# Linear attention ahead of two MLPs: the product with the state in four 64x64 parts, behind the state's own product

## The chip, the core and the metric

One core of a Trainium2 chip runs the whole program. The metric is the device time of one execution in microseconds (us); the inputs lie in HBM when it starts, and the output lies there when it ends. TensorE (PE) multiplies matrices and writes its results to PSUM; VectorE (DVE), ScalarE (ACT) and GpSimd (POOL) work element by element; SyncE (SP) issues the DMAs. [...]

## What is computed

The output of a causal linear attention with decay goes, token by token, through two MLPs. Only the attention is touched by the change. There are 2 batches of 8 heads, 768 tokens and 64 channels per head:

```python
for b in range(nb):
    intra = einsum(qb, kb) * Dmask          # scores inside a block
    intra = einsum(intra, vb)
    inter = einsum(qb * lam_pow, kv_state)  # the product with the state
    out[block] = intra + inter
    kv_state = lam_block * kv_state + einsum(kb * rev_pow, vb)
x = out as (1536 tokens, 512 features)
h = relu(x @ w_in); x = (s * h * h + b) @ w_out                   # first MLP, 2048 wide
x = rmsnorm(x); y = (silu(x @ w_gate) * (x @ w_val)) @ w_out2     # second MLP, 1536 wide
```

The kernel uses blocks ("chunks") of 128 tokens in place of 64, which gives the same result: 6 chunks per batch, 12 in all, numbered g = 0 to 11; chunk 0 and chunk 6 begin a batch with an empty state, and chunks 5 and 11 end one and leave no state behind.

## The kernel before, in words

The attention stage is a loop over the chunks, in `attention_moe_moe2_kernel`. Two heads share the 128 partitions ("a pair"): the upper 64 partitions hold the channels of an even head, the lower 64 those of an odd one. In each round g, the program gives TensorE this work, in this order (the order is written out by hand, and no scheduler changes it):

- `outputs(g)`, first part (line 558, tile `o`): values times masked scores, 8 products, one per head, with 128 tokens on the rows of the array and 64 channels on its columns (the trace writes 128*64), into one PSUM bank. Even and odd heads go to the two halves of the array's columns.
- `outputs(g)`, second part (line 567, tile `o`): the product with the state, 4 products, one per pair, 128*128. The state of a pair stands as a 128x128 block with the two heads' 64x64 states on its diagonal and zeros elsewhere. It adds to the same bank. Chunks 0 and 6 don't have it.
- `outputs(g)`, third part (line 584, tile `st`): the chunk's share of the new state, 8 products 128*64 of k scaled (`kdec`) with v. Chunks 5 and 11 don't have it.
- `scores(g + 2)` (line 516, tile `sc`): the scores of the chunk after the next, 8 products with 64 channels on the rows (64*128), into two banks.

The other engines work around it. ACT copies the bank `o` to x (line 578, one 128x512 operation; x of a batch is `xq`), and makes `kdec` of the next chunk (line 535, eight 128x64 operations, one per head). POOL makes q scaled (`qs`, line 530, 128x512) for the next chunk and scales the old state (line 546, 128x512). DVE adds the new share to the state (line 597, two 64x256 operations) and masks the scores of chunk g + 2 (`prob`, line 518, two 128x512 operations). The bank of `o` alternates between 4 and 5 with g, so a chunk's products need the copy of the chunk before the last.

From chunk 4 on, the loop also carries tasks for the first MLP, by a table `plan` keyed by g: splits of x into a high and a low part (lines 143 on ACT and 146 on DVE), and the unpacking of the first two blocks of weights (`w_tasks`). Unpacking reads a block that SP has fetched (line 116, a `st` buffer of 512 KB), takes two words from it on ACT (lines 123 and 129), shifts and adds them on DVE (lines 135 and 140), splits off the high part on ACT (line 143, 128x1024, tile `u`) and the low part on DVE (line 146). These tasks stand in the engines' queues between those of the attention. In round 11, two products of the first MLP (`hquad(0)`, line 295, tile `h`) stand ahead of `outputs(11)`.

SP issues the loads in order: chunk g + 4's q, k and kv (lines 442, 445, 450) at the end of round g, each as soon as its buffer is free; the kv buffer is free when chunk g's `st` is done. The first two blocks of weights (512 KB each, 4 KB per partition) go in behind chunk 8's loads, ahead of chunk 9's.

Of the kernel before, what the change touches and what calls it, by code (L numbers as in the profile page):

```python
# [15 lines left out]
P = 128  # L16
# [6 lines left out]
def attention_moe_moe2_kernel(  # L23
# [89 lines left out]
    raw = {}  # L113
# [60 lines left out]
    def load_w(j, part):  # L174
        if j < NPR:
            n = 4 * j + 2 * (1 - part)
        else:
            n = NU1 + 3 * (j - NPR) + 1 - part
        raw[j, part] = fetch(n, part)
# [150 lines left out]
    def hbanks(i):  # L330
        places = (7, 0, 6, 4) if i == 0 else tuple(4 * ((i + 1) % 2) + j for j in range(4))
        return [bank(n, f"h{i}_{j}")[:, 0:HB] for j, n in enumerate(places)]
# [104 lines left out]
    with tc.tile_pool(name="att", bufs=1) as att:  # L437
# [67 lines left out]
        qs, prob, state, o_bank = {}, {}, {}, {}  # L505
# [32 lines left out]
        def prepare_state(g):  # L538
            c = g % NCH
            if c == NCH - 1:  # L540
                return
            sn = att.tile([P, NPAIR, P], F32, tag="state", bufs=2, name=f"state{g}")
            if c == 0:
                nc.gpsimd.memset(sn, 0.0)
            else:
                nc.gpsimd.tensor_tensor(
                    sn, state[g - 1], lpow[:, :, P - 1 : P].to_broadcast([P, NPAIR, P]), op=ALU.mult
                )
            state[g] = sn

        def outputs(g):
# [3 lines left out]
            o = bank(4 + g % 2, f"o{g}")  # L555
            for h in range(H):
                pr = slice(h % 2 * D, (h % 2 + 1) * D)
                nc.tensor.matmul(  # L558
                    o[pr, h // 2 * P : (h // 2 + 1) * P],
                    vn[:, h, :],  # L560
                    prob[g][:, h, :],
                    start=h < 2,
                    stop=c == 0 and h >= H - 2,
                    skip_group_check=True,
                )
            for p in range(NPAIR if c else 0):
                nc.tensor.matmul(  # L567
                    o[:, p * P : (p + 1) * P],
                    state[g - 1][:, p],
                    qs[g][:, p],  # L570
                    start=False,
                    stop=p == NPAIR - 1,
                    skip_group_check=True,
                )
            o_bank[g] = o
            o3 = o.rearrange("p (a i) -> p a i", i=P)
            tok = slice(c * P, (c + 1) * P)
            nc.scalar.activation(xq[g // NCH][:, :, tok], o3, AF.Copy)
            if not last:
# [7 lines left out]
                return st  # L587
            return None

        def add_state(g, st):  # L590
            if st is None:
                return
            st3 = st[:, 0 : NPAIR * D].rearrange("p (a i) -> p a i", i=D)
            sn = state[g]
# [591 lines left out]
```

## Time and profile before

| | |
|---|---|
| device time, median of 3 runs | 594.74 us (594.52 to 595.35) |
| span of the profiled execution, first to last instruction | 592.7 us |
| attention stage in that execution, up to TensorE's long run of MLP products | 0 to 55.8 us |
| TensorE busy | 586.4 us, 99% of the span |
| DVE, ACT, POOL busy | 407.8, 321.5, 114.5 us |
| moved by DMA | 52 MB; 264 GB/s over the first 60 us |

The span is that of one execution, with times counted from its start. The time of a run is from outside and about 2 us more than a span, so a saving in the span is taken as the same saving in the time. In the trace a matmul of these types appears as two instructions (a product of two passes), so 8 products are 16 rows. Each row has a start and a duration; matmuls overlap, so the time of a group is read from its start to the start of the next group.

### The profile page before, as it was taken

Reading aid. Unit: us, or ns where it says so; the run is one execution under the profiler, and the core shown is the slowest. Engines: PE = TensorE matmul, PEld = TensorE weight load, DVE = VectorE, ACT = ScalarE, POOL = GpSimd, SP = SyncE. Lnnn points to the kernel's source line nnn. Section 1 sums busy time; section 2 is a strip of 40 time slices with the busy share of each in tenths; the row PEclk is TensorE's granted clock in tenths of the full one; section 3 lists DMA queues with packets and bytes.
Section 4 is the critical chain, followed back from the end, with each engine's and each line's share of the span. In section 5 each row is a group of like instructions: output and inputs, shape, how many; then the busy total and the mean of one; then the engine's idle time right before and its main releaser. Section 6 shows DMA issues by size and latency. Waiting matters only on the chain.

```text
span 592.7 us, 9212 instructions
## 1 busy us (share of the span) xinstructions
PE 586.4 (99%) x3590; PEld 543.1 (92%) x3590; DVE 407.8 (69%) x654; ACT 321.5 (54%) x572; POOL 114.5 (19%) x118
## 2 busy tenths in 40 slices
PE   9999999999999999999999999999999999999997
PEld 8888999999998888988888999999999998888886
DVE  6587957777777775769947986777777777874200
ACT  5677977777776663646542434444444445763200
POOL 3550032223103232041311002222222200000000
PEclk9999999999999999999999999999999999999999
DMA  8992202223223441221120001221222212320310
GB/s 312 334 350 72 72 1 78 77 72 131 72 72 110 139 143 35 71 69 38 36 72 1 1 2 71 72 72 71 72 72 71 86 58 77 136 72 1 142 38 35
DMA packets 17282, 51.98 MB, mean 88 GB/s; under 512 B 2390, under 2 KB 2390, under 8 KB 17238
## 3 DMA queue, kind: packets, MB, share of 16 engines
q1 hardware_dynamic: 17238, 51.39, 25.4%
q8 instruction: 28, 0.46, 0.3%
q14 instruction: 16, 0.13, 0.1%
HBM read 48.24 MB, written 3.15 MB: 87 GB/s over the span
## 4 chain that ended last, share of the span: by engine, by line
PE 93%; DVE 3%; ACT 2%; issue 1%; DVEq 0%
PE q L295 28%; PE h L295 17%; PE out L1078 17%; PE y L795 15%; PE z L807 8%; PE sc L516 2%; PE o L558 2%; PE o L567 2%; PE st L584 1%; PE warm L481 1%; PE rb L775 0%; DVE r_None L306 0%; PE nps L758 0%; DVE u_None L140 0%; ACT u_None L143 0%
## 5 line engine op out<-in xcount | busy, mean ns | idle before, releaser
L143 ACT ACTIVATE u_None<-u_None 128x768 fp32r<-128x768 f32 (+2 forms) x50 | 42.9, 871 | 55.0 <-DVE u_None L140 48.7
L295 PE MATMUL q<-u0b_None,u_None 128*128 128x384 f32 x360 | 68.4, 336 | 0.0
L295 PEld LDWEIGHTS q<-u0b_None,u_None 128*128 128x128 f32 x360 | 62.8, 188 | 0.6 <-DVE st_None L306 0.3
L146 DVE TENSOR_TENSOR u_None<-u_None,u_None 128x512 fp32r<-128x512 f32 (+1 forms) x66 | 54.1, 845 | 11.0 <-ACT u_None L143 11.0
L218 POOL TENSOR_TENSOR u_None<-u_None 128x256 f32<-128x256 f32 x18 | 19.9, 1103 | 188.6 <-DVE u_None L140 188.6
L295 PE MATMUL q<-xs_None,u_None 128*128 128x384 f32 x288 | 55.3, 334 | 0.0
L123 ACT ACTIVATE u_None<-st_None 128x512 f32<-128x512 f32 x68 | 45.2, 664 | 17.2 <-issue 14.3
L140 DVE CUSTOM_DVE_ANT_0 u_None<-u_None 128x1024 uint16<-128x1024 uint16 x68 | 47.8, 703 | 5.0
L295 PEld LDWEIGHTS q<-xs_None,u_None 128*128 128x128 f32 x288 | 50.4, 188 | 0.0
L129 ACT ACTIVATE u_None<-st_None 128x512 uint32<-128x512 uint16 x68 | 45.3, 666 | 5.1 <-DVE u_None L146 5.1
L306 DVE TENSOR_TENSOR st_None<-q,r_None 128x384 f32<-128x384 f32 x48 | 26.6, 553 | 18.8 <-PE q L295 18.7
L972 ACT ACTIVATE st_None<-r_None 128x384 f32<-128x384 f32 x24 | 12.6, 526 | 47.3 <-DVE r_None L306 47.3
L1078 PE MATMUL out<-u_None,xs_None 128*128 128x512 f32 x144 | 32.8, 389 | 0.0
L1078 PEld LDWEIGHTS out<-u_None,xs_None 128*128 128x128 f32 x144 | 27.0, 188 | 5.6
L1085 DVE COPY st_None<-out 128x512 f32<-128x512 f32 x4 | 2.8, 692 | 40.9 <-PE out L1078 40.9
L135 DVE TENSOR_SCALAR u_None<-u_None 128x512 uint32<-128x512 uint32 x68 | 30.1, 443 | 0.4
L424 POOL TENSOR_TENSOR wsum_None<-wsum_None,u_None 128x512 f32<-128x512 f32 x15 | 20.6, 1377 | 49.0 <-DVE u_None L140 49.0
L295 PE MATMUL q<-u0a_None,u_None 128*128 128x384 f32 x144 | 29.0, 335 | 0.2 <-DVE st_None L306 0.2
L295 PE MATMUL q<-g_None,u_None 128*128 128x384 f32 x144 | 26.9, 334 | 0.0
L295 PEld LDWEIGHTS q<-u0a_None,u_None 128*128 128x128 f32 x144 | 25.3, 188 | 0.5 <-DVE st_None L306 0.5
L1078 PE MATMUL out<-u_None,u0b_None 128*128 128x512 f32 x108 | 25.3, 389 | 0.0
L295 PEld LDWEIGHTS q<-g_None,u_None 128*128 128x128 f32 x144 | 25.1, 188 | 0.0
(202 smaller groups left out, 1310.4 us busy)
## 6 DMA issues: line engine op xcount, KB each, us to landing
st_None<-in_w_dram SPq DMA_DIRECT2D x68, 512.0 KB, 3.3
kv<-in_kv_dram SPq DMA_DIRECT2D x12, 512.0 KB, 6.3
q<-in_qT_dram SPq DMA_DIRECT2D x12, 256.0 KB, 6.8
k<-in_kT_dram SPq DMA_DIRECT2D x12, 256.0 KB, 6.5
out_dram<-st_None SPq DMA_DIRECT2D x8, 256.0 KB, 2.0
out_dram<-u_None SPq DMA_DIRECT2D x4, 256.0 KB, 2.1
row<-in_lam_dram SPq DMA_DIRECT2D x1, 0.0 KB
g_col<-in_rms_g_dram SPq DMA_DIRECT2D x1, 2.0 KB, 3.5
```

The source lines that it names most:

```text
L123: nc.scalar.activation(m, t[:, :, 1].bitcast(F32), AF.Prelu, scale=2.0**-112, alpha=-(2.0**32))
L129: nc.scalar.activation(to.bitcast(U32), low, AF.Copy, scale=2.0**-13)
L135: nc.vector.tensor_scalar(m, m, 3, None, op0=ALU.logical_shift_left)
L140: nc.vector.tensor_tensor(m, m, t.bitcast(U32), op=ALU.add)
L143: nc.scalar.activation(to, src, AF.Copy)
L146: nc.vector.tensor_tensor(to, src, hi.bitcast(F32), op=ALU.subtract)
L295: nc.tensor.matmul(ps, ws[:, wi, wop * KC + kt * P : wop * KC + (kt + 1) * P], xs[xop][:, xi, kt, :], start=n == 0 and not more, stop=n == ...
L306: nc.vector.tensor_tensor(to, ps, more, op=ALU.add)
L424: nc.gpsimd.tensor_tensor(wsum, wsum, m, op=ALU.add)
L795: nc.tensor.matmul(acc[d], wt[:, wi, d * P : (d + 1) * P], gt[:, gi, 0:BT], start=it == 0 and pi == 0, stop=it == NF1 - 1 and pi == 2,)
L807: nc.tensor.matmul(acc2[d // 2][:, d % 2 * BX : (d % 2 + 1) * BX], wt[:, wi, d * P : (d + 1) * P], gt[:, gi, BT:BW], start=it == 0 and pi ...
L1078: nc.tensor.matmul(ps, rows_[:, ai], w_out[f][:, wi, :], start=first and pi == 0, stop=last and pi == 2)
```

## The change

**The state.** A pair's state is kept as two 64x64 blocks (tile 128 x 4 x 64 in place of 128 x 4 x 128, without the zeros). The product with the state becomes 8 products, one per head, each with 64 channels on the rows and 64 on the columns of the array; the heads' order (0, 2, 1, 3, 4, 6, 5, 7) lets four that follow each other use the four quarters of the array. It moves behind the `st` products. Scaling the old state on POOL has half the elements, and DVE's addition is one operation in place of two (for a batch's first chunk a copy; POOL's clearing of the state falls away).

**The banks of `o`.** [...] The two tiles are made once, ahead of the loop. The copy to x is two operations of 128x256, one per bank. The first quad of MLP products uses bank 1 in place of bank 4.

**The order of x's features.** Heads land in x in another order (a tile of x holds the heads of one bank). To match it, the rows of the first MLP's first weights are fetched in that order: each 512 KB block by four DMAs of 128 KB in runs of 1 KB, in place of one DMA in runs of 4 KB (16 blocks).

**`kdec`.** Heads 4 to 7 are made by one POOL operation (128x256), which stands ahead of `qs` in POOL's queue; ACT makes heads 0 to 3, four operations in place of eight.

```diff
     def load_w(j, part):
         if j < NPR:
-            n = 4 * j + 2 * (1 - part)
+            src = w32[4 * j + 2 * (1 - part)].rearrange("(b p) (a c x) -> c p b a x", b=2, a=2, c=2)
+            to = stage[part].rearrange("(c p) (b a x) t -> c p b a (x t)", c=2, b=2, a=2)
+            for c in range(2):
+                for b_ in range(2):
+                    nc.sync.dma_start(to[c, :, b_], src[c, :, b_])
+            raw[j, part] = stage[part]
...
-        places = (7, 0, 6, 4) if i == 0 else tuple(4 * ((i + 1) % 2) + j for j in range(4))
+        places = (7, 0, 6, 1) if i == 0 else tuple(4 * ((i + 1) % 2) + j for j in range(4))
...
         def prepare(g):
             c = g % NCH
+            if c < NCH - 1:
+                kd = att.tile([P, H, D], F32, tag="kdec", bufs=2, name=f"kdec{g}")
+                half = slice(H // 2, H)
+                nc.gpsimd.tensor_tensor(
+                    kd[:, half], kvt[g][:, 0, half], dec[:, half, P - 1 : P].to_broadcast([P, H // 2, D]), op=ALU.mult
+                )
+                for h in range(H // 2):
+                    nc.scalar.activation(kd[:, h, :], kvt[g][:, 0, h, :], AF.Copy, scale=dec[:, h, P - 1 : P])
+                qs[g, "kd"] = kd
             if c:
                 t = att.tile([P, NPAIR, P], F32, tag="qs", bufs=2, name=f"qs{g}")
                 nc.gpsimd.tensor_tensor(t, qt[g], lpow, op=ALU.mult)
                 qs[g] = t
-            if c < NCH - 1:
-                kd = att.tile([P, H, D], F32, tag="kdec", bufs=2, name=f"kdec{g}")
-                for h in range(H):
-                    nc.scalar.activation(kd[:, h, :], kvt[g][:, 0, h, :], AF.Copy, scale=dec[:, h, P - 1 : P])
-                qs[g, "kd"] = kd
...
+        o_banks = [bank(4 + i, f"o_{i}") for i in range(2)]
+
+        def o_block(g, h):
+            pr = slice(h // 2 % 2 * D, (h // 2 % 2 + 1) * D)
+            return o_banks[h % 2][pr, (2 * (g % 2) + h // 4) * P : (2 * (g % 2) + h // 4 + 1) * P]
...
-            o = bank(4 + g % 2, f"o{g}")
-            for h in range(H):
...
-            for p in range(NPAIR if c else 0):
+            for n, h in enumerate((0, 2, 1, 3, 4, 6, 5, 7)):
                 nc.tensor.matmul(
-                    o[:, p * P : (p + 1) * P],
-                    state[g - 1][:, p],
-                    qs[g][:, p],
...
+                    o_block(g, h), vn[:, h, :], prob[g][:, h, :], start=n < 4, stop=c == 0 and n >= 4,
                     skip_group_check=True,
                 )
-            nc.scalar.activation(xq[g // NCH][:, :, tok], o3, AF.Copy)
...
+            for n, h in enumerate((0, 2, 1, 3, 4, 6, 5, 7) if c else ()):
+                pr = slice(h % 2 * D, (h % 2 + 1) * D)
+                nc.tensor.matmul(
+                    o_block(g, h), state[g - 1][pr, h // 2], qs[g][pr, h // 2], start=False, stop=n >= 4,
+                    skip_group_check=True,
+                )
+            tok = slice(c * P, (c + 1) * P)
+            for i in range(2):
+                o3 = o_banks[i][:, 2 * (g % 2) * P : 2 * (g % 2 + 1) * P].rearrange("p (a i) -> p a i", i=P)
+                nc.scalar.activation(xq[g // NCH][:, 2 * i : 2 * i + 2, tok], o3, AF.Copy)
+            return st
 
         def add_state(g, st):
...
-            for hf in range(2):
-                pr = slice(hf * D, (hf + 1) * D)
-                nc.vector.tensor_tensor(sn[pr, :, pr], sn[pr, :, pr], st3[pr], op=ALU.add)
+            if g % NCH:
+                nc.vector.tensor_tensor(state[g], state[g], st3, op=ALU.add)
+            else:
+                nc.vector.tensor_copy(state[g], st3)
```

**Where instructions move: TensorE, rounds 9 and 10.** First the kernel before, from the products of chunk 9's `o` on (`prob10` and `kv10` are its scores and its k and v, `state9` the state that chunk 9 left), up to the first MLP's first product:

```order
L558 MATMUL o9_698<-prob9_601,kv9_507 64x128 x8
L567 MATMUL o9_698<-qs9_624,state8_635 128x128 x4
L584 MATMUL st9_712<-kv9_507,kdec9_626 64x64 x8
...
L558 MATMUL o10_743<-prob10_662,kv10_561 64x128 x8
L567 MATMUL o10_743<-qs10_685,state9_696 128x128 x4
L584 MATMUL st10_757<-kv10_561,kdec10_687 64x64 x8
L295 MATMUL h0_0_772<-u0b_1_None_67,u2_3_None_69 128x384 x12
```

Now the same place in the changed program (lines 570, 580 and 585 are 558, 584 and 567 of before, line 300 is 295):

```order
L570 MATMUL o_0_148<-prob10_661,kv10_560 64x128 x2
L570 MATMUL o_1_149<-prob10_661,kv10_560 64x128 x2
...
L580 MATMUL st10_756<-kv10_560,kdec10_690 64x64 x8
L585 MATMUL o_0_148<-qs10_696,state9_698 64x128 x2
L585 MATMUL o_1_149<-qs10_696,state9_698 64x128 x2
...
L300 MATMUL h0_0_783<-u0b_1_None_67,u2_3_None_69 128x384 x12
```

The product with the state stands behind `st`, twice as many instructions, and the tiles `o_0` and `o_1` are the same in every chunk: the first products of a chunk wait for both copies of the chunk before it.

**ACT, rounds 8 to 10.** Before, from the copy of chunk 8 to that of chunk 10 (`u1_2` is where the weights are unpacked, `u2_3` where the split goes):

```order
L578 ACTIVATE xq1_6_None_72<-o8_637 128x4x128
L129 ACTIVATE u1_2_None_68<-st0_11_None_77 128x512
L143 ACTIVATE u2_3_None_69<-u1_2_None_68 128x1024
L535 ACTIVATE kdec10_687<-kv10_561,dec_135 128x64 x8
L578 ACTIVATE xq1_6_None_72<-o9_698 128x4x128
L143 ACTIVATE u0b_1_None_67<-xq0_5_None_71 128x768
L578 ACTIVATE xq1_6_None_72<-o10_743 128x4x128
```

And now, from the copies of chunk 8 to those of chunk 9 (lines 540 and 592 are 535 and 578 of before):

```order
L592 ACTIVATE xq1_6_None_72<-o_0_148 128x2x128
L592 ACTIVATE xq1_6_None_72<-o_1_149 128x2x128
L129 ACTIVATE u1_2_None_68<-st0_11_None_77 128x512
L143 ACTIVATE u2_3_None_69<-u1_2_None_68 128x1024
L540 ACTIVATE kdec10_690<-kv10_560,dec_135 128x64 x4
L592 ACTIVATE xq1_6_None_72<-o_0_148 128x2x128
L592 ACTIVATE xq1_6_None_72<-o_1_149 128x2x128
```

The order of the kinds is the same, with four `kdec` operations fewer and two copies for one: the copies of chunk 9 stand behind the split of the weights and chunk 10's `kdec`.

**POOL, rounds 8 to 10.** Before, and behind it the changed program (lines 536, 544 and 553 are the new `kdec`, and 530 and 546 of before):

```order
L530 TENSOR_TENSOR qs9_624<-q9_503,lpow_147 128x512
L546 TENSOR_TENSOR state8_635<-state7_574,lpow_147 128x512
L530 TENSOR_TENSOR qs10_685<-q10_557,lpow_147 128x512
L546 TENSOR_TENSOR state9_696<-state8_635,lpow_147 128x512
L530 TENSOR_TENSOR qs11_739<-q11_618,lpow_147 128x512
L546 TENSOR_TENSOR state10_741<-state9_696,lpow_147 128x512
```

```order
L536 TENSOR_TENSOR kdec10_690<-kv10_560,dec_135 128x256
L544 TENSOR_TENSOR qs10_696<-q10_556,lpow_147 128x512
L553 TENSOR_TENSOR state9_698<-state8_631,lpow_147 128x256
L544 TENSOR_TENSOR qs11_744<-q11_617,lpow_147 128x512
L553 TENSOR_TENSOR state10_746<-state9_698,lpow_147 128x256
```

One operation more per chunk, ahead of `qs`, and the state's has half the elements.

## Rows read from the trace of the kernel before

**Rows 1.** The page's part 2: granted clock, 40 slices of 14.8 us.

```profile
PEclk9999999999999999999999999999999999999999
```

**Rows 2.** Chain of waits, in order of time: start us, us, what (x instructions).

```profile
20.16 1.02 PE o L558 x16
21.18 1.09 PE o L567 x8
22.27 0.61 PE st L584 x16
...
32.03 0.46 PE st L584 x16
...
36.31 1.09 PE sc L516 x16
```

**Rows 3.** TensorE's timeline at 20.09 us: start us, us, what.

```profile
20.09 0.33 PE L558 MATMUL o<-prob,kv 128*64 128x128 f32 x2
```

**Rows 4.** TensorE's timeline, round 10; in brackets idle time before and its releaser.

```profile
44.97 1.09 PE L558 MATMUL o<-prob,kv 128*64 128x128 f32 x16
46.33 1.13 PE L567 MATMUL o<-qs,state 128*128 128x128 f32 x8 [0.26 <-DVE state L597]
47.39 1.42 PE L584 MATMUL st<-kv,kdec 128*64 128x64 f32 x16
```

**Rows 5.** ACT's copies out of PSUM, lines 578 and 346 (ns, least/median/most).

```profile
L578 ACT ACTIVATE xq_None<-o x12: 570/588/599, 12.4 to 55.3; 128x512 f32<-128x512 f32 x12
...
L346 ACT ACTIVATE u_None<-h x4: 466/468/487, 55.8 to 80.7; 128x384 f32<-128x384 f32 x4
```

**Rows 6.** ACT's timeline, rounds 8 to 10.

```profile
45.45 1.06 ACT L143 ACTIVATE u_None<-u_None 128x1024 fp32r<-128x1024 f32 x1 [3.98 <-DVE u_None L140]
46.42 2.01 ACT L535 ACTIVATE kdec<-kv,dec 128x64 f32<-128x64 f32 x8
48.33 0.58 ACT L578 ACTIVATE xq_None<-o 128x512 f32<-128x512 f32 x1
```

**Rows 7.** DVE's timeline, rounds 7 to 9.

```profile
39.20 0.69 DVE L140 CUSTOM_DVE_ANT_0 u_None<-u_None 128x1024 uint16<-128x1024 uint16 x1
...
41.25 1.29 DVE L518 TENSOR_TENSOR prob<-sc,dec 128x512 f32<-128x512 f32 x2
...
43.32 0.42 DVE L135 TENSOR_SCALAR u_None<-u_None 128x512 uint32<-128x512 uint32 x1
43.88 1.54 DVE L140 CUSTOM_DVE_ANT_0 u_None<-u_None 128x1024 uint16<-128x1024 uint16 x1
```

**Rows 8.** POOL's timeline at that time; line 218's operations (ns, least/median/most).

```profile
43.42 1.45 POOL L530 TENSOR_TENSOR qs<-q,lpow 128x512 f32<-128x512 f32 x1 [1.10 <-PE o L567]
...
L218 POOL TENSOR_TENSOR u_None<-u_None x18: 726/1352/1392, 68.2 to 463.3; 128x256 f32<-128x256 f32 x18
```

**Rows 9.** SP's issues, and the time to landing of chunk 9's k.

```profile
27.15 0.90 SPq L116 DMA_DIRECT2D st_None<-in_w_dram  x2
...
28.57 0.48 SPq L445 DMA_DIRECT2D k<-in_kT_dram  x1
...
DMA to landing us min/median/max: 7.5/7.5/7.5
```

**Rows 10.** Busy time by stretch: PE, PEld, DVE, ACT, POOL, PEclk, DMA share, GB/s.

```profile
21.00:28.00 7.00, 7.00 (x105) 6.10 (x102) 3.61 (x8) 2.63 (x7) 4.34 (x5) 1.00 0.84 289
29.00:41.00 12.00, 12.00 (x184) 10.73 (x183) 9.04 (x17) 11.41 (x36) 6.22 (x5) 1.00 1.00 383
```

**Rows 11.** Timelines of DVE and TensorE: the first Strassen quad's last input, its reader.

```profile
79.99 2.15 DVE L146 TENSOR_TENSOR u_None<-u_None,u_None 128x768 fp32r<-128x768 f32 x3
...
85.10 2.24 PE L295 MATMUL h<-u0b_None,u_None 128*128 128x384 f32 x12
```

**Rows 12.** Chain of waits in the first 10 us.

```profile
1.10 2.50 PE warm L481 x10
...
9.85 1.12 PE o L558 x16
```

More of the change, by code (lines that the diff above doesn't have):

```diff
@@ L175, in load_w @@
         if j < NPR:
-            n = 4 * j + 2 * (1 - part)
-        else:
-            n = NU1 + 3 * (j - NPR) + 1 - part
-        raw[j, part] = fetch(n, part)
+            src = w32[4 * j + 2 * (1 - part)].rearrange("(b p) (a c x) -> c p b a x", b=2, a=2, c=2)
[4 more added lines that the diff above has]
+            raw[j, part] = stage[part]
+        else:
+            raw[j, part] = fetch(NU1 + 3 * (j - NPR) + 1 - part, part)
     m_late = {}
@@ L503, in scan_lpow @@
             nc.vector.memset(neg_half, -0.5)
-        qs, prob, state, o_bank = {}, {}, {}, {}
+        qs, prob, state = {}, {}, {}
         def scores(g):
@@ L541, in prepare_state @@
                 return
[L542 to L545, printed above, removed]
+            sn = att.tile([P, NPAIR, D], F32, tag="state", bufs=2, name=f"state{g}")
+            if c:
                 nc.gpsimd.tensor_tensor(
-                    sn, state[g - 1], lpow[:, :, P - 1 : P].to_broadcast([P, NPAIR, P]), op=ALU.mult
+                    sn, state[g - 1], lpow[:, :, P - 1 : P].to_broadcast([P, NPAIR, D]), op=ALU.mult
                 )
             state[g] = sn
+        o_banks = [bank(4 + i, f"o_{i}") for i in range(2)]
+        def o_block(g, h):
+            pr = slice(h // 2 % 2 * D, (h // 2 % 2 + 1) * D)
+            return o_banks[h % 2][pr, (2 * (g % 2) + h // 4) * P : (2 * (g % 2) + h // 4 + 1) * P]
         def outputs(g):
@@ L554, in outputs @@
             last = c == NCH - 1
-            o = bank(4 + g % 2, f"o{g}")
-            for h in range(H):
-                pr = slice(h % 2 * D, (h % 2 + 1) * D)
+            for n, h in enumerate((0, 2, 1, 3, 4, 6, 5, 7)):
                 nc.tensor.matmul(
[L559 to L563, printed above, removed]
+                    o_block(g, h), vn[:, h, :], prob[g][:, h, :], start=n < 4, stop=c == 0 and n >= 4,
                     skip_group_check=True,
                 )
-            for p in range(NPAIR if c else 0):
-                nc.tensor.matmul(
-                    o[:, p * P : (p + 1) * P],
-                    state[g - 1][:, p],
-                    qs[g][:, p],
[L571 to L577, printed above, removed]
-            nc.scalar.activation(xq[g // NCH][:, :, tok], o3, AF.Copy)
+            st = None
             if not last:
@@ L586, in outputs @@
                     )
-                return st
-            return None
+            for n, h in enumerate((0, 2, 1, 3, 4, 6, 5, 7) if c else ()):
[9 more added lines that the diff above has]
+            return st
         def add_state(g, st):
@@ L593, in add_state @@
             st3 = st[:, 0 : NPAIR * D].rearrange("p (a i) -> p a i", i=D)
-            sn = state[g]
-            for hf in range(2):
-                pr = slice(hf * D, (hf + 1) * D)
-                nc.vector.tensor_tensor(sn[pr, :, pr], sn[pr, :, pr], st3[pr], op=ALU.add)
+            if g % NCH:
+                nc.vector.tensor_tensor(state[g], state[g], st3, op=ALU.add)
+            else:
+                nc.vector.tensor_copy(state[g], st3)
         scores(0)
```

## The prediction

> **What bounds the kernel now.** [...] Then the chain of waits: over the attention stage it is a string of TensorE groups, each starting where the one before ended, so what TensorE's queue holds there is what counts. One chunk of the steady part costs 1.02 us for o, 1.09 for the product with the state, 0.61 for st [rows 2] and 1.09 for the scores, 3.81 in all. Two more readings of these rows: st costs 0.46 when it stands directly behind o (chunk 6, which has no product with the state), so a change of the array's shape costs some 0.15; and o's rows come two at one start [rows 3], so its 16 passes run in pairs: 8 rounds in 1.02 us, which is 8 x 0.109 and 0.15 for the change of shape. Then the timelines of TensorE, ACT, DVE and POOL around round 10, where two of its groups come late, and SP's issues with the landing of the loads.
>
> **The change, part by part.**
>
> *The product with the state.* Each product fills a quarter of the array. If four run at once as o's two do, 16 passes take 4 rounds: 4 x 0.109 + 0.15 = 0.59 in place of 1.09. That the passes can be issued so closely is in st's row: 16 in 0.46 us. st now stands behind o, in the same shape, and costs 0.46 in place of 0.61. The gain is 0.50 + 0.15 = 0.65 in the 8 chunks with both, 0.50 in chunks 5 and 11: 8 x 0.65 + 2 x 0.50 = **-6.2**. No row shows four at once. The upper bound of its cost is a run in pairs (8 rounds, 1.02), the lower is issue alone (0.46). I take 0.59: two tiles beside each other (o) and two above each other (the scores, 16 passes in 1.09) both reach full pairs in these rows.
>
> *Round 10's old waits.* o of chunk 10 ends at 44.97 + 1.02 = 45.99, the product with the state starts at 46.33 (0.34, DVE's state was late), and st takes 1.42 where 0.61 is usual, waiting for ACT's kdec [rows 4]. Both lie behind the new wait that follows and are swallowed by it: **-1.1**.
>
> *The new wait on the copies.* Before, a chunk's o needed the copy of the chunk before the last. Now the two tiles are the same in every chunk, so o of chunk g + 1 waits for both copies of chunk g. A copy of 128x256 I estimate at 0.35, on the line through 0.468 at 384 columns and 0.588 at 512 [rows 5]; two are 0.7. Between a chunk's last product and the next o stand the scores, 1.09: in most rounds the copies fit. In round 10 they don't. ACT has the copies of chunk 9 behind a split of weights (line 143) that waited 3.98 us for DVE, and behind kdec of chunk 10 [rows 6]. DVE comes to what it waits for only behind the masking of chunk 10's scores: from the start of that, 41.25, to the split's start, 45.45, it is 4.20 us [rows 7]. Then 0.97 for the split (45.45 to 46.42), 1.0 for four kdec (half of 2.01) [rows 6] and 0.7 for the copies: 6.9 us from the end of chunk 10's scores to the release of its o. TensorE's own work in that time is o, st and the product with the state of chunk 9 and the scores of chunk 11: 1.02 + 0.46 + 0.59 + 1.09 = 3.16. So it would wait 3.7. To this comes that TensorE is there sooner than before while DVE, whose unpacking of weights (line 140) ended only 1.36 us ahead of the masking [rows 7], follows the weights and not TensorE: between 0 and 1.4 later, I take 0.5. **+4.2**. Bounds: in the 4.20 us lies one collision. DVE's line 140 took 1.54 in place of 0.69 while POOL ran qs from 43.42 on [rows 7, 8]. Without it the wait is 2.9; with one more of that size, since POOL now has kdec ahead of qs, and the 0.5, it is 5.1.
>
> [...]
>
> *Loads.* By round 8 TensorE is ahead by 5 x 0.65 + 0.50 = 3.75 us (chunks 1 to 4, 7, and 5) and wants chunk 9's scores at 36.31 - 3.75 = 32.56 [rows 2]. Chunk 9's k landed at 28.57 + 7.5 = 36.1, 0.2 ahead of its use [rows 9]. It stands behind 1 MB of weights in SP's queue, now 8 issues of some 0.45 in place of 2. In 21 to 28 us DMA moved 289 GB/s against 383 later [rows 10], so of the bytes ahead of k at most (383 - 289) / 383 x 7 = 1.7 us can be won: landing at 34.4. If all loads simply follow TensorE's earlier release of the buffers (2.6 us, chunks 1 to 4), 33.5. That makes a wait of 0.9 to 1.9; the shorter runs of the weights (1 KB) may add up to 2.7 us (1 MB at 383 GB/s moved at half the rate), and, below, smaller transfers may let k through sooner, 0. I take the low end, **+1.0**, range 0 to 2.5, as the issues of SP (8 x 0.45 = 3.6) don't delay k beyond that.
>
> *Work that lies beside TensorE, at nothing.* POOL's kdec (128x256, between half of qs's 1.45 and 0.726, line 218's least [rows 8]) is made up for by the state's halved operation. DVE's one addition, ACT's second copy (0.1 more than one copy) and four kdec fewer lie in slack outside round 10. In the next stage TensorE is led by no one until the first Strassen quad, whose last input DVE ends at 79.99 + 2.15 = 82.14, read at 85.10 [rows 11]: 3.0 us of slack, over the net gain. So what the stage gains arrives at the end.
>
> **Sum**: -6.2 - 1.1 + 4.2 + 1.0 = **-2.1**. The working uses the profiled execution (span 592.7); runs are timed some 2 us above the span, and I take the same difference off the median: 594.74 - 2.1 = **592.6**.
>
> **The rivals.**
>
> *S, slower: the wait costs TensorE its clock.* Ahead of chunk 10's o TensorE would stand still for 3.7 to 4.2 us, longer than anywhere in this stage. At the start of the run, behind an idle first microsecond, its passes took 250 ns (10 in 2.50 us [rows 12]) against 136 for the same shape later (8 in 1.09 [rows 2]), up to the first o, at 9.85: 8.7 us at about half the speed, a loss of 4.3. If the wait brings that back in full, the time is 592.6 + 4.3 = 596.9. It decides from about 3.3 us of loss on. Against it: the page shows the upper level even over those first microseconds [rows 1], and no wait of this kernel is long enough to tell. [...]
>
> *P, pairs only.* If the quarters above each other don't run together with those beside each other, the product takes 1.02: the gain is (0.07 + 0.15) x 8 + 0.07 x 2 = 1.9. The wait on the copies shrinks by the 0.43 that TensorE's own work is longer, to 3.8, and k is in time: -1.9 - 1.1 + 3.8 = +0.8, 595.5. For it: no row shows both kinds at once; against it: each kind alone reaches its full rate.
>
> *D, wait and loads both at their upper ends*: -7.3 + 5.1 + 2.5 = +0.3, 595.0, within 0.2% of before. For it speaks POOL's longer queue, against it that a late k puts off the scores and with them the start of the wait, so that the two overlap in part.
>
> *N, the wait is short*: -7.3 + 2.9 + 0 = -4.4, 590.3; this is the lower end of the forecast's own case, not a case apart. It needs POOL out of DVE's way.
>
> **How the numbers follow.** A measurement of this kernel can tell a difference of about 0.2%, 1.19 us, from none: faster means below 593.55, slower above 595.93. The forecast (four at once, a wait of some 4 us) has a chance of 0.58, its own range is 590.2 to 594.9, and 0.05 of it lies within 0.2%. S has 0.15, of which 0.02 lies within 0.2%; P 0.14, of which 0.10 does and 0.03 is slower; D 0.13, nearly all of it within 0.2%. Faster: 0.58 - 0.05 = 0.53, with the rest of P 0.54; slower: 0.13 + 0.03 = 0.16; the same: 0.30. The range goes from 590.2, the forecast's lower end, to 596.2, which takes in D and P and the smaller part of S.
>
> **What the profile after would show.** Right: line 585's groups at 0.59 us and st at 0.46; a chunk of the steady part at 3.16 us; one long idle time of TensorE, ahead of chunk 10's o, of 3 to 5 us, released by ACT's copy (line 592), with the split and kdec just ahead of it on ACT; a wait of 0 to 2.5 ahead of chunk 9's scores, ended by a DMA. Wrong: line 585 at 1.0 (P); passes of 250 ns behind the wait (S); waits on the copies in every round, which would mean that the copies take longer than the scores; or a gain of 7 us, which would mean that I misread the tiles' reuse or that ACT reaches the copies earlier than I think. If DVE's last split for the Strassen quad comes later than TensorE wants it, the gain is given back at some 80 us.

## The result, and the profile after

| | before | changed |
|---|---|---|
| device time, median (range), 4 runs each | 594.63 us (594.26 to 595.35) | 599.51 us (597.62 to 599.74) |
| span of the profiled execution | 592.7 us | 598.0 us |
| TensorE's long run of MLP products starts at | 55.84 us | 60.60 us |

The ratio is 1.0074, 95% interval 1.0058 to 1.0091: the change is slower by 4.9 us, where 2.1 us of gain were forecast, and the range ended at 596.2. All of it but some 0.5 us arises in the attention stage: the MLPs' long run starts 4.76 us later, its later products between 4.7 and 5.0 us later, the last of them 4.81. The spans differ by 5.3 us; the rest lies behind the last product.

TensorE's timeline of the changed kernel, rounds 7 to 11 (columns as in [rows 4]; line 570 is o, 580 st, 585 the product with the state, 521 the scores, 300 the MLP's products):

```profile
32.34 0.67 PE L585 MATMUL o<-qs,state 64*64 64x128 f32 x16
36.60 1.34 PE L521 MATMUL sc<-q,k 64*128 64x128 f32 x16 [3.59 <-DMA k<-in_kT_dram]
37.88 1.97 PE L570 MATMUL o<-prob,kv 128*64 128x128 f32 x16
39.64 1.07 PE L580 MATMUL st<-kv,kdec 128*64 128x64 f32 x16
40.63 0.75 PE L585 MATMUL o<-qs,state 64*64 64x128 f32 x16
41.31 1.16 PE L521 MATMUL sc<-q,k 64*128 64x128 f32 x16
42.41 1.09 PE L570 MATMUL o<-prob,kv 128*64 128x128 f32 x16
43.33 0.64 PE L580 MATMUL st<-kv,kdec 128*64 128x64 f32 x16
43.89 0.67 PE L585 MATMUL o<-qs,state 64*64 64x128 f32 x16
44.49 1.16 PE L521 MATMUL sc<-q,k 64*128 64x128 f32 x16
49.69 1.98 PE L570 MATMUL o<-prob,kv 128*64 128x128 f32 x16 [4.04 <-ACT xq_None L592]
51.46 1.07 PE L580 MATMUL st<-kv,kdec 128*64 128x64 f32 x16
52.45 1.13 PE L585 MATMUL o<-qs,state 64*64 64x128 f32 x16
53.52 2.82 PE L300 MATMUL h<-u0b_None,u_None 128*128 128x384 f32 x12
...
58.34 1.09 PE L570 MATMUL o<-prob,kv 128*64 128x128 f32 x16
```

Groups are read from start to start. In the steady part (42.41 to 45.58) o takes 0.92 us, st 0.56, the new product 0.60 and the scores 1.09. The chain of waits, from which [rows 2] come, divides o and st otherwise, at the same sum:

```profile
18.94 1.02 PE o L570 x16
19.96 0.46 PE st L580 x16
20.43 0.60 PE o L585 x16
```

The new product's first four passes start at one time (43.89 to 43.91 us):

```profile
43.89 0.34 PE L585 MATMUL o<-qs,state 64*64 64x128 f32 x4
```

In the timeline stand two long waits, where the longest of [rows 4] was 0.26: 3.59 us ahead of chunk 9's scores, ended by a DMA, and 4.04 ahead of chunk 10's o, ended by ACT's copy. Behind each of them the same passes take almost twice as long: o 1.76 us in place of 0.92, st 0.99 in place of 0.56. The stretches show the clock with it (columns as in [rows 10]):

```profile
35.00:40.00 5.00, 3.40 (x40) 3.21 (x42) 1.94 (x4) 2.63 (x8) 0.85 (x2) 0.74 0.99 369
40.00:45.00 5.00, 5.00 (x102) 4.35 (x100) 3.26 (x6) 1.38 (x4) 5.00 (x6) 0.91 1.10 288
45.00:50.00 5.00, 0.96 (x16) 0.77 (x16) 4.86 (x7) 2.63 (x8) 2.40 (x3) 0.77 0.60 118
50.00:55.00 5.00, 5.00 (x54) 4.55 (x51) 1.49 (x4) 2.02 (x5) 0.00 (x0) 0.55 0.00 0
55.00:60.00 5.00, 5.00 (x53) 4.41 (x51) 3.31 (x6) 2.58 (x4) 0.00 (x0) 1.00 0.30 97
```

Granted are 0.55 to 0.91 of full speed on average from 35 to 55 us, and 1.00 in the stretches before and behind them. By single microseconds it is 0.50 from 38 to 40 and from 48 to 54 us, 1.00 from 41 to 47 and from 55 on, and lies between the two only at the turns (0.57 to 0.84).

The account, from these starts: the product and st give 6.2 and the old waits of round 10 1.1, as forecast. Against it stand the wait for the load (from 32.94, where the product before ends, to 36.60: 3.7), slow passes behind it (36.60 to 41.31, 4.71 us for 3.17 us of work: 1.5), the wait on the copy (45.58 to 49.69: 4.1) and slow passes behind it (49.69 to 58.34, 8.65 us, where o and st with 1.48, the new product with 0.60 and the MLP's products with the 4.37 of before, 48.73 to 53.10 in its timeline, make 6.45: 2.2), and 0.3 at chunk 6's scores. That is +4.5 of the 4.76 measured; the rest isn't assigned.

Why the load is late is in SP's timeline, with the chain's row for chunk 8's kv:

```profile
23.68 0.33 SPq L455 DMA_DIRECT2D kv<-in_kv_dram  x1
24.06 7.42 SPq L181 DMA_DIRECT2D st_None<-in_w_dram  x8
31.58 1.32 SPq L447 DMA_DIRECT2D q<-in_qT_dram  x1
32.95 0.43 SPq L450 DMA_DIRECT2D k<-in_kT_dram  x1
```

```profile
23.68 7.25 DMA kv<-in_kv_dram
```

The eight DMAs of weights took SP 7.42 us, not 3.6, and chunk 9's k was issued at 32.95, 4.4 us later than in [rows 9]. It landed 3.5 us after its issue, at 36.5, and so 0.4 later than before (36.1), while TensorE was there 3.3 us sooner (32.94 against 36.24): its lead became the wait. The program's order with the semaphores that each DMA waits for (`st` the weights, `kv_456` chunk 8's kv) shows eight in turn:

```
L455 DMA kv_456<-in_kv_dram 128x1024 [waits DMAHW3_49,PE_49,Activation_49]
L181 DMA st_11_None<-in_w_dram 64x2x256 [waits DMAHW4_49]
...
L181 DMA st_11_None<-in_w_dram 64x2x256 [waits DMAHW3_49]
L447 DMA q_506<-in_qT_dram 128x512 [waits DMAHW4_49,Pool_49]
```

The eighth DMA of weights has the semaphore of chunk 8's kv, and is issued only when that has landed, at 23.68 + 7.25 = 30.93:

```profile
30.94 0.53 SPq L181 DMA_DIRECT2D st_None<-in_w_dram  x1
```

The first seven take 5.47 us, at some 0.6 each and 1.57 for the sixth (why that one is long stays open), and SP then stands still for 1.4 until the eighth. So the 7.42 us are 6.0 of issues, where 3.6 were counted, and 1.4 of waiting for a semaphore. In the trace of e2 below the eighth goes at 30.42, with kv's landing at 30.41, in that of e10 at 29.78, with 29.76.

### The profile page after: what moved, and what is told of

It is laid out like the page before. It is cut to its first block, busy times and chain, and to the rows that moved or that the text cites. A ratio compares the mean times of both kernels' runs of the same rounds, so it can differ in the third digit from the quotient of the medians.

```text
span 598.0 us, 9431 instructions
## 1 busy us (share of the span) xinstructions
PE 583.8 (98%) x3670; PEld 541.0 (90%) x3670; DVE 406.1 (68%) x644; ACT 313.3 (52%) x544; POOL 116.4 (19%) x126
## 3 DMA queue, kind: packets, MB, share of 16 engines
HBM read 48.24 MB, written 3.15 MB: 86 GB/s over the span
## 4 chain that ended last, share of the span: by engine, by line
PE 90%; DVE 3%; DMA 2%; ACT 2%; issue 1%; POOL 1%; SPq 0%; POOLq 0%; ACTq 0%; DVEq 0%
PE q L300 28%; PE h L300 17%; PE out L1083 16%; PE y L800 15%; PE z L812 8%; DMA kv<-in_kv_dram 2%; PE o L570 1%; PE sc L521 1%; PE warm L486 1%; DVE u_None L140 1%; PE o L585 1%; PE st L580 1%; PE rb L780 0%; DVE r_None L311 0%; PE nps L763 0%
```

## The experiments

"Slower" and "faster" are against the kernel before, run beside each; medians lie between 594.5 and 594.7 for it.

**What holds the loads.** Four runs cut the blocks of weights in other ways; the first two blocks are those of the attention stage. All four, and e11 and e12 below, leave out the reordering of the weights' rows, so their output is not the reference's, and they say something of the time alone.

```diff
-            for c in range(2):
-                for b_ in range(2):
-                    nc.sync.dma_start(to[c, :, b_], src[c, :, b_])
+            raw[j, part] = fetch(4 * j + 2 * (1 - part), part)                 # e1
...
+            for i in range(4):                                                 # e2
+                r = slice(32 * i, 32 * (i + 1))
+                nc.sync.dma_start(stage[part].rearrange("p c t -> p (c t)")[r], src[r])
...
+            for a_ in range(2):                                                # e9
+                nc.sync.dma_start(to[:, a_], src[:, a_])
...
+            for a_ in range(2):                                                # e10
+                for c in range(2):
+                    nc.sync.dma_start(to[:, a_, c], src[:, a_, c])
```

> This run fetches each 512 KB block of weights by one DMA in runs of 4 KB again; the weights' rows are then not in the order of x's heads. Theory Q (SP has eight semaphores for its DMAs, taken in turn, so a ninth DMA is issued only when the first of the eight has landed; eight DMAs of weights fill them): chunk 9's k is issued at about 25.5 us instead of 32.95 and lands by 33.5; TensorE's wait ahead of chunk 9's scores falls from 3.6 to under 1 us and the slow passes behind it (1.5 us lost) are gone: 599.5 - 2.7 - 1.5 = 595.3, down to 594.3. Theory R (runs of 1 KB hold the DMA engines up): the same. Theory B (the bytes ahead of k set its landing, however they are cut): the wait stays above 3 us, 599.5.

> This run fetches each block of weights by four DMAs of 32 partitions in runs of 4 KB; the weights' rows are not in the order of x's heads. So there are eight DMAs as in the changed kernel, but long runs. Theory Q: SP is held for some 7 us as in the changed kernel, the wait ahead of chunk 9's scores stays at 3 to 4 us, 599 to 600. Theory R: the wait goes as with one DMA per block, 595. Theory B: 599.5 in both runs.

> The first two blocks of weights by two DMAs each, of all 128 partitions, in runs of 1 KB as in the changed kernel; the weights' rows are not in the order of x's heads. Theory P (a DMA that writes to only 64 or 32 partitions moves some 190 GB/s, as the two earlier runs with such DMAs did from 27.4 us on, and one of 128 partitions some 390, whatever its runs): the rate stays at 350 to 400 GB/s in 24 to 33 us, the wait ahead of chunk 9's scores is under 1.2 us, 594.5 to 596. Theory R (runs of 1 KB are what is slow): 190 to 250 GB/s, a wait of 2 to 4 us, 598 to 600.

> As the run before, but by four DMAs a block, each of all 128 partitions with one run of 1 KB: eight DMAs, as in the changed kernel; the weights' rows are not in the order of x's heads. Theory P alone: as the run before, 594.5 to 596. Theory Q beside it (eight semaphores in turn): the last of the eight and chunk 9's q and k are issued only when chunk 8's kv has landed, near 30 us, k lands near 34, the wait ahead of chunk 9's scores is 1 to 2.5 us, 596 to 598.5.

Measured: one DMA a block 594.93 (ratio 1.0005, 0.9994 to 1.0015); eight of 32 partitions with runs of 4 KB 600.43; four of all partitions with runs of 1 KB 595.78; eight of all partitions 597.90. The stretch from 28 to 32 us, in that order:

```profile
28.00:32.00 4.00, 4.00 (x76) 3.69 (x76) 3.00 (x5) 3.30 (x10) 2.92 (x4) 1.00 0.98 370
```

```profile
28.00:32.00 4.00, 4.00 (x76) 3.69 (x74) 3.02 (x5) 2.67 (x9) 1.63 (x3) 1.00 0.89 207
```

```profile
28.00:32.00 4.00, 4.00 (x82) 3.69 (x80) 3.69 (x6) 3.04 (x9) 2.86 (x3) 1.00 1.06 368
```

```profile
28.00:32.00 4.00, 4.00 (x76) 3.69 (x75) 3.23 (x6) 3.23 (x10) 2.77 (x3) 1.00 0.81 246
```

and the changed kernel itself:

```profile
28.00:32.00 4.00, 4.00 (x80) 3.69 (x78) 3.54 (x6) 2.16 (x7) 1.37 (x3) 1.00 0.97 176
```

The last column is GB/s. Runs of 1 KB are not what is slow: with all partitions they move 368. With DMAs of 64 partitions among the loads it is 176, with those of 32 partitions 207, while the DMA engines are busy at 0.97 and 0.89. (e10's 246 stands beside a share of 0.81: the engines were less busy, with SP held until 30.10 us.) So at runs of 1 KB the 64 partitions have 0.48 of the rate of all (176 of 368), and at runs of 4 KB the 32 partitions 0.56 (207 of 370); why the rate falls so, the traces don't show. Eight DMAs in place of four cost 597.90 - 595.78 = 2.1 us with full partitions: SP is held for 5.68 us in e10, and the wait ahead of chunk 9's scores is back:

```profile
24.42 5.68 SPq L183 DMA_DIRECT2D st_None<-in_w_dram  x8
```

```profile
35.65 2.08 PE L523 MATMUL sc<-q,k 64*128 64x128 f32 x16 [2.33 <-DMA k<-in_kT_dram]
```

With one DMA a block that wait is 0.59 and with four 0.96, both with no slow passes behind. So theories Q and P hold together, R and B fall: from 0.96 (four DMAs) the wait grows to 2.33 with eight and to 3.59 with eight half-filled ones. By the medians the last step costs 599.51 - 597.90 = 1.6 us, but the intervals of these two overlap. In e2 the wait was 1.30 with 0.78 at the next chunk, less than theory Q said, though the time was as it said; its three unprofiled runs, 1.8 to 3.3 us longer than the profiled one, had a lower mean granted clock (0.989 to 0.991 against 0.994).

**What holds chunk 10's o, and the clock.**

```diff
-            8: [xt["lB12"]] + w0[2:4], 9: [xt["hB22"]] + w0[4:5], 10: ...
+            8: [xt["lB12"]] + w0[2:3], 9: w0[3:4] + [xt["hB22"]] + w0[4:5], 10: ...   # e3
+            if g == 10:                                                               # e4
+                idle = bank(0, "idle")
+                for i in range(14): nc.tensor.matmul(idle[:, 0:P], ones, ones, start=True, stop=True)
             st = outputs(g)
```

> The split of the weights (line 143 with DVE's sum ahead of it) moves from round 8 to round 9, so that on ACT the copies of chunk 9 stand ahead of it. Theory C (the copies stand behind the split in ACT's queue, and the split behind DVE): the wait ahead of chunk 10's o falls from 4.0 to under 1 us, and the slow passes behind it (2.2 us lost) go as well: 599.5 - 3.1 - 2.2 = 594.2, down to 593.2. Rival (POOL's kdec and qs, not ACT's queue, hold the round up): wait and time stay, 599.5, or fall by less than 1 us.

> 14 products of ones with ones (28 passes, some 3.8 us) go to a bank that nobody reads, ahead of chunk 10's o, so that TensorE works through the wait. Theory K (the wait lets the clock fall): o, st and the product with the state of chunk 10 run at 1.02, 0.46 and 0.60 us and the first h products at their usual 0.17 a pass: 599.5 - 2.2 = 597.3. Rival (those passes are slow for their operands' sake, since DVE, POOL and ACT all work there): they stay slow, 599.5.

e3: 598.25, a gain of 1.3 us, where 5 to 6 were expected. The wait ahead of chunk 10's o is gone from the trace, so theory C holds for the wait; in its place stand two at the first products of the MLP, and the slow passes behind the untouched load wait last longer (scores 2.08):

```profile
36.42 2.08 PE L521 MATMUL sc<-q,k 64*128 64x128 f32 x16 [3.60 <-DMA k<-in_kT_dram]
...
49.70 0.62 PE L300 MATMUL h<-u0b_None,u_None 128*128 128x384 f32 x2 [0.97 <-ACT u_None L143]
51.03 2.01 PE L300 MATMUL h<-u0b_None,u_None 128*128 128x384 f32 x10 [0.71 <-DVE u_None L146]
```

Its profiled run (596.33) is near the lowest of six that reach to 599.12, so the trace, whose long run of MLP products starts 3.3 us earlier than the changed kernel's, shows more gain than the median. The six runs differ in the mean granted clock, from 0.997 (596.04 us) to 0.990 (598.38 to 599.12): how long the lower clock lasts changes from run to run, and the interval of the ratio (1.0039 to 1.0073) reaches 1 us to either side of the median.

e4: 597.58, 1.9 faster than the changed kernel by the medians, whose intervals overlap, 2.2 expected. TensorE works through the wait, and o behind it is back near its usual time (0.97 us from start to start, 0.92 usual, 1.77 in the changed kernel), at a granted clock of 1.00:

```profile
45.92 3.39 PE L646 MATMUL idle<-ones 128*128 128x128 f32 x28
49.38 1.14 PE L570 MATMUL o<-prob,kv 128*64 128x128 f32 x16
...
55.90 1.09 PE L570 MATMUL o<-prob,kv 128*64 128x128 f32 x16
```

```profile
50.00:55.00 5.00, 5.00 (x62) 4.76 (x59) 3.15 (x6) 3.23 (x7) 0.00 (x0) 1.00 0.02 7
```

From chunk 10's o to chunk 11's it is 6.52 us in place of 8.65. Nothing else was changed, so the passes were slow for TensorE's standing still, as theory K has it. The wait itself was not shortened.

**The order within the new product.** The table of heads becomes (0, 4, 2, 6, 1, 5, 3, 7).

> The changed kernel with the products with the state in the order of heads 0, 4, 2, 6, 1, 5, 3, 7: two that follow each other use the same quarter of the array. If passes start strictly in the order of issue, a quarter's second product holds up the next quarter's: 0.60 becomes 0.8 to 1.05 us a chunk, 2 to 4.5 us in ten chunks, some of it inside the waits: 601 to 603. If passes for a free quarter overtake: 0.60, 599.5.

One run, 600.59, which is too few to read a time from. The product takes 0.62 us (44.91 to 45.53 in its timeline), against 0.60, and its passes, too, start four at a time (between 44.91 and 44.96 us):

```profile
44.91 0.36 PE L585 MATMUL o<-qs,state 64*64 64x128 f32 x4
```

```profile
44.91 0.69 PE L585 MATMUL o<-qs,state 64*64 64x128 f32 x16
45.53 1.16 PE L521 MATMUL sc<-q,k 64*128 64x128 f32 x16
```

In this order the program's first four passes are all for one quarter. The trace doesn't name a pass's quarter, but four of them for one quarter would be some 0.11 us apart, if the quarter took them one by one, by the 0.109 us that the prediction worked out for a round of o. By that estimate passes for a free quarter overtook here, ahead of the program's order, and the order of heads matters little (0.62 us against 0.60).

**Both losses taken away, and the product's place.** e11 has e1's weights, and in round 9 the split ahead of chunk 11's scores; e12 has line 585 ahead of line 580 as well.

```diff
-            8: [xt["lB12"]] + w0[2:4], 9: ...
+            8: [xt["lB12"]] + w0[2:3], 9: ...
...
             add_state(g, st)
+            if g == 9:
+                w0[3]()
             scores(g + 2)
```

> One DMA per block as in the first run (the weights' rows are not in the order of x's heads), and the split of the weights in round 9, ahead of chunk 11's scores. Both waits are then gone: 594.9 less 4.3 (the wait ahead of chunk 10's o) less 2.7 (slow passes behind it), plus 0.5 to 1.7 of waits ahead of the first h products: 588.4 to 589.6. Rival (the next stage gives the gain back, because DVE's last split for the first Strassen quad ends 3.0 us before it is read): 591 to 592.

> As the run before, with the product with the state ahead of st again. If only the changes of the array's shape count: 0.15 more in each of the 8 chunks that have both, 1.2 us more than the run before. Rival (it waits for the state, which DVE finishes late): 2 to 5 us more.

e11: 591.04, ratio 0.9938 (0.992 to 0.9957), faster than before by 3.7 us, and above the 588.4 to 589.6 that were expected. Its long run of MLP products starts at 51.95, 5.4 earlier than in e1's trace (57.38), at the lower end of the sum's 5.3 to 6.5; but e1's profiled run was the slowest of its ten (596.52), so the sum should have started there and not at the median. The time lies where the rival had it, but not for its reason: the next stage gives next to nothing back, since the last product starts 3.87 us earlier than before, and the long run 3.89. What is left are two waits at the first h products:

```profile
44.33 0.61 PE L297 MATMUL h<-u0b_None,u_None 128*128 128x384 f32 x2 [0.86 <-ACT u_None L143]
45.66 2.03 PE L297 MATMUL h<-u0b_None,u_None 128*128 128x384 f32 x10 [0.72 <-DVE u_None L146]
```

e12: 592.84, 1.8 more. The product ahead of st costs 0.15 a chunk in the trace (a chunk takes 3.32 in place of 3.17), 1.2 in eight; the rest lies within the runs' spread.

**Trials of a faster kernel with the reference's result.** All of these have the weights in the order of x's heads.

```diff
-            if g == 4:
+            if 3 <= g < 7:             # e5 to e7: two DMAs a round
+            if g in (4, 5):            # e14, e15, e17: four a round;  e16: (5, 6)
-                    nc.sync.dma_start(to[c, :, b_], src[c, :, b_])
+                    nc.sync.dma_start(to[:, b_, a_], src[:, :, b_, a_])                   # e13, e14
+                    (nc.scalar if c and not j else nc.sync).dma_start(to[c, :, b_], ...)  # e17
```

> The eight DMAs of the first two blocks of weights are issued two at a time, behind the loads of rounds 3 to 6, in place of all eight in round 4. The result is the reference's. Theory Q (eight semaphores, in turn): chunk 9's loads are no longer held, the wait ahead of its scores falls from 3.6 to under 1 us as in the run with one DMA per block, and the time is 594 to 595.5; the wait ahead of chunk 10's o stays at some 4.2 us with slow passes behind it. Rival (each round's two more DMAs put off the chunks' loads): waits of up to 1.5 us ahead of the scores of chunks 7, 8 or 9, 596 or more.

> As the run before, and the split of the weights (DVE's sum and ACT's line 143) moves to round 9, ahead of chunk 11's scores, so that ACT has the copies of chunk 9 ahead of it. If both waits are what the losses came from: 594.9 less 4.3 (the wait) less 2.7 (the slow passes behind it, 9.19 us from chunk 10's o to chunk 11's in the run with one DMA per block, 6.45 usual), plus 0.5 to 1.7 of waits ahead of the first h products: 588.5 to 589.7, 589.2 as the likeliest. Rival (the gain isn't let through: DVE ends the last split for the first Strassen quad 3.0 us before it is read, and the stage would end 5 us earlier): up to 2.3 us given back there, 591.5.

> As the run before, with all of kdec on ACT again. Theory A (ACT is short of time: 2.0 us of kdec, 0.65 of copies and 0.84 of a split are 3.5 us in a round of 3.17, more where weights are unpacked): st waits for kdec in rounds 4 to 10, 1 to 3 us in all, 590.2 to 592.2. Rival (POOL's kdec costs what it saves, because DVE's sums stretch from 0.7 to 1.5 us beside POOL): the same time or less, 588 to 589.2.

Measured 599.94, 601.42 and 600.30: e5's rival was right, with waits of 1.51 and 1.92 us at chunks 8 and 9, and the sums of e6 and e7, which rest on waits that would be gone, fail with it. Half-filled DMAs stand among every round's loads, the rate is 246 to 290 GB/s from 24 to 40 us in e5 and e6, and chunks 8, 9 and 10 wait in turn (2.52, 0.42 and 2.38 us in e6). On such a base e7 says little of kdec's place, which stays open: 1.1 faster than e6, at overlapping intervals.

> The weights in the order of x's heads, by four DMAs a block as in the changed kernel, but each of all 128 partitions (the rows of both halves of a run of 1 KB in one DMA); ACT's split of the weights (line 143 alone, not DVE's sum) in round 9, behind the copies of chunk 9. The result is the reference's. By the run with eight DMAs of all partitions (597.9): the wait ahead of chunk 9's scores stays at some 2 us with 1.7 us of slow passes behind it, the wait ahead of chunk 10's o and its slow passes go (4.1 and 2.2), about 0.5 us of waits ahead of the first h products: 592.1, between 591 and 593. Rival (with the first wait still there the second comes back elsewhere): 595 or more.

> As the run before, with four of the eight DMAs in round 4 and four in round 5, so that chunk 9's loads stand behind four of them only. The result is the reference's. Theory Q with P: chunk 9's q and k are issued at about 27 us, the wait ahead of chunk 9's scores falls to some 1 us without slow passes, chunk 10's scores wait 0 to 1.5: 589.5 to 591.5. Rival (as with two DMAs a round, each round's loads come late, because eight DMAs in flight hold fewer bytes): waits of over 1.5 us at chunks 9 and 10 both, 593 to 595.

668.68 and 669.21: neither theory. To fill all partitions, the source's outermost step became one of two:

```profile
28.00:32.00 4.00, 4.00 (x76) 3.69 (x74) 3.14 (x6) 2.56 (x9) 2.91 (x4) 1.00 0.17 56
```

A share of 0.17 of the 16 engines, with 56 GB/s, comes to 2.7 of them at work on average (0.17 x 16). e10, with as many DMAs of all partitions in runs of 1 KB, but with the 128 partitions as the outermost step, has a share of 0.81 and 246 GB/s in the same stretch. That the step of two is the cause is the author's reading; no run changed the step alone.

> The changed kernel's own DMAs of weights (64 partitions each), the first block's four in round 4 and the second's four in round 5, and the split of the weights (with DVE's sum) in round 9 ahead of chunk 11's scores. The result is the reference's. If order is what counts (chunk 9's q and k stand behind four such DMAs only): k is issued near 27.3 us, lands near 34, a wait of 1 to 2 us ahead of chunk 9's scores and 0 to 2 ahead of chunk 10's, no or short slow passes: 592 to 594.5, 593 as the likeliest. Rival (half-filled DMAs in the way of every chunk, as with two a round): waits of over 2 us at both, with slow passes, 597 to 601.

> As the run before, one round later (rounds 5 and 6), with the unpacking's first two steps a round later too. The result is the reference's. Chunk 9's loads are ahead of all weights: no wait there; chunk 10's scores wait 1 to 2 us, chunk 11's 0 to 2, and the first h products 1.6 to 3 us for the weights: 592.5 to 595. Rival: as above, 597 to 601.

> As the run with the two blocks in rounds 4 and 5, but the DMAs that write the lower 64 partitions are issued from ACT's queue and those for the upper 64 from SP's, so that halves of both kinds can be under way at once. The result is the reference's. If that fills both halves (theory P): 340 to 390 GB/s in 28 to 36 us in place of 225 to 276, waits of under 1.2 us ahead of the scores of chunks 9 and 10, 591 to 593. Rival (the two queues are served one after the other, or ACT is held by its DMAs): 225 to 280 GB/s, waits as in that run, 595 to 598.

596.08 (1.0028, 1.0014 to 1.0043), 595.99 (1.0015, 0.9994 to 1.0035) and 595.77 (1.0014, 1.0001 to 1.0027): 3.4 to 3.7 us better than the changed kernel, none better than before. The loss moves with the DMAs: in e15 chunk 10's scores wait 3.15 us, in e16 those of chunks 10 and 11 wait 3.03 and 3.92. Two queues don't bring the rate of whole DMAs (251 GB/s from 28 to 32 us, 225 in e15). ACT was idle for 3.40 us up to 31.98, a wait that the trace has ended by a load of q, and issued the last two of its four DMAs in that time, at 30.62; it made the copies of chunk 6 only from 32.95 on, and chunk 7's o waited for them:

```profile
33.37 1.98 PE L570 MATMUL o<-prob,kv 128*64 128x128 f32 x16 [2.53 <-ACT xq_None L592]
```

No version with the reference's result was faster than the kernel before. Not tried: bringing the weights' halves to their places by other means than a DMA.

## Why the prediction was wrong

- **The product with the state and st: right.** 0.60 and 0.46 us in the chain of waits against 0.59 and 0.46, a chunk of 3.17 against 3.16, and four passes start at once. Rival P falls; by e8 (0.62 us) not even the order of heads is needed for it.
- **The wait on the copies: right in place and cause, and in size partly by luck.** 4.04 us against 4.2, released by line 592. e3 and e11 remove it by moving the split on ACT, with DVE's sum ahead of it, to round 9, and leave POOL's order as it was; which of the two moves does it was not separated. As in [rows 7], the DVE operation ahead of the split ran beside POOL's qs and took 1.53 us. The 0.5 that the text added for DVE's weights is right by luck: DVE was idle for 1.74 us ahead of 42.30 us and not behind the weights, and what came on top is line 135, 0.84 us in place of 0.42 beside POOL's scaling of the state (44.05 to 45.38):

```profile
44.83 0.84 DVE L135 TENSOR_SCALAR u_None<-u_None 128x512 uint32<-128x512 uint32 x1
45.80 1.53 DVE L140 CUSTOM_DVE_ANT_0 u_None<-u_None 128x1024 uint16<-128x1024 uint16 x1
```

- **Loads: the first step that failed.** "I take the low end, +1.0, range 0 to 2.5, as the issues of SP (8 x 0.45 = 3.6) don't delay k beyond that." It was 3.7. The step priced SP's issues at 0.45 us each, where they took 0.6 and more, and left out that each waits for the DMA eight places ahead of it, which the program's order shows and which cost 1.4 us at the eighth; and it put a halved rate, an estimate that no row of before shows, down to short runs, which cost little (e9: 368 GB/s, a wait of 0.96), and not to half-filled DMAs, with which the rate was about half (176 of 368 GB/s). With one DMA a block the same wait is 0.59, with four whole ones in all 0.96: there the +1.0 holds. So the term was mis-sized by 2.7 us, for causes that the text didn't have.
- **The clock: the second step that failed, put at nothing in the forecast's sum.** Rival S, at 0.15, happened, and twice. It cost 2.2 us behind the wait that the text named (2.1 by e4's trace) and 1.5 behind the load wait, 3.7 in all. The price in the text, 4.3, was the whole of the first 8.7 us; a single fall cost 1.5 to 2.8 us in the traces (2.8 in e2, 2.7 in e1). The argument against S, the upper level in [rows 1] over the first microseconds, was empty: the trace's first entry of the clock is at 10.0 us, and the stretches ahead of it read 1.00 (every microsecond from 0 to 10) with no entry behind them. With the load term right the forecast's own case would still have been no gain: with the terms of e1's trace it is -6.2 - 1.1 + 4.3 + 0.6 + 2.7 = +0.3. That e1's median is +0.3 as well (594.93 against 594.67) is in part luck, for the trace is of its slowest run, and has early waits of 0.97 and 0.55 us that this sum leaves out. The likeliest case should have carried the clock: the prediction itself had read passes of 250 ns in place of 136 behind an idle first microsecond [rows 12], and put a wait of some 4 us ahead of chunk 10's o. With TensorE at work through that wait, in e4, this o took 0.97 us in place of 1.77.
- **The next stage: right.** Of the stage's end, 3.89 us earlier in e11, 3.87 arrive at the last product.
- The sum with what was measured: -6.2 - 1.1 + 4.1 + 2.2 + 3.7 + 1.5 + 0.3 = +4.5, against -2.1 forecast. Of these 6.6 us the clock makes 3.7 and the load term 2.7; 0.3 are at chunk 6's scores. The time lay outside the range since the range held one of the two causes at a time: loads at their end (D), or the clock (S), not both, though the clock fell behind either wait.

## What to carry to other kernels

Three things went with the cost of a DMA that was cut into more pieces: the wait for the landing of the DMA eight places ahead, which held what stood behind it (1.4 us at the eighth piece), the partitions that each piece filled (176 and 207 GB/s with 64 and 32 of them, 368 with all), and the outermost step of its source (56 GB/s with a step of two). The same bytes in 2, 4 and 8 pieces of all partitions took 594.9, 595.8 and 597.9 us, and in 8 pieces of 64 or 32 partitions 599.5 and 600.4. When a faster TensorE meets a fixed deadline of another engine, its gain turns into a wait, and a wait can cost twice, as here: its own length, 4.1 us, and slow passes behind it, 2.2. Price both in the likeliest case.

## What the runs showed that was not expected

- Eight small DMAs ahead of a load held SP for longer than their issues: 7.42 us in the changed kernel, of which 1.4 are a wait for the landing of the DMA eight places ahead.
- From 28 to 32 us the rate was 176 and 207 GB/s with DMAs of 64 and of 32 partitions, and 368 and 370 with those of 128, at runs of 1 and of 4 KB.
- With an outermost step of two: 54 to 56 GB/s from 28 to 36 us in e13, and 74 us on the kernel, all of whose 16 blocks come that way.
- How long TensorE stands still doesn't alone say whether its clock falls. In e5 a wait of 1.92 us was followed by o at 1.97 us (granted 0.71 on average from 36 to 40 us), in e15 one of 3.15 us by o at 1.09 (granted 0.999 over the whole execution). (In e5 a wait of 1.51 us ends 5.2 us ahead of that one's end, in e15 one of 1.17 us 6.4 us ahead.) What decides was not tried.

```profile
37.18 1.66 PE L522 MATMUL sc<-q,k 64*128 64x128 f32 x16 [1.92 <-DMA k<-in_kT_dram]
38.77 1.97 PE L571 MATMUL o<-prob,kv 128*64 128x128 f32 x16
```

```profile
41.23 1.16 PE L521 MATMUL sc<-q,k 64*128 64x128 f32 x16 [3.15 <-DMA k<-in_kT_dram]
42.32 1.09 PE L570 MATMUL o<-prob,kv 128*64 128x128 f32 x16
```
